# Five small loads into an unread tile, in a decode layer with attention and an MLP

## The chip, the cores and the metric

The kernel runs on one core of a Trainium2 chip, with one launch. The metric is device time in microseconds (us); the figure for the kernel before is the median of three runs. Beside them stands one execution that the hardware profiler recorded. Engines are TensorE (PE; its weight loads are PEld), VectorE (DVE), ScalarE (ACT), GpSimd (POOL) and SyncE (SP). SP and ACT issue the DMAs of this kernel; a "q" behind an engine's name (SPq) means its instruction queue.

## What is computed

One token `x` of width 1024 is normalised, and then goes two ways whose results are added to it: attention over the last 4096 positions of a cache, with 32 query heads on 4 key/value heads, and an MLP of width 3584.

```python
xn  = layernorm(x)                                   # 1 x 1024
q   = xn @ wq                                        # 1024 x 4096
p   = softmax(q . k_cache[last 4096] * 128**-0.5)    # 32 heads, 4 kv heads
o   = (p . v_cache[last 4096]).reshape(1, 4096)
a   = o @ wo                                         # 4096 x 1024
b   = gelu(layernorm(xn) @ w1 + b1) @ w2 + b2        # 1024 x 3584, 3584 x 1024
out = x + a + b
```

With one token every weight is used once. In bf16 the caches, `wq`, `wo`, `w1` and `w2` come to nearly 40 MB, all of which must be loaded.

## The kernel before

All large operands go through four SBUF buffers of 32 KB per partition (`ring`, lines 56 to 64). SP issues their loads in this order: `k_sb` in four loads (line 72), `wq` in two (81), `w1` in two (207), `v_sb` in three (213), `w2` in two (221), `wo` in six (229). The first half of `wo` is one load of 16 rows for each partition; the second half is cut into 8, 4, 2, 1 and 1 rows, so that the last rows can be used one by one. ACT issues three small loads at the start (lines 102 to 104): `x`, `b2` and `b1`, each into a single partition. A load from `w1` on can be issued only when a buffer has been released by the work that read it.

The work follows the loads. DVE transposes the keys in blocks (186); DVE and ACT copy them in order (200, 202); PE makes `q` (238), the MLP's first layer (258), the scores (276) and the attention output (320). Then 56 matmuls of `w2` and 56 of `wo` accumulate in PSUM (341). The last four rows of `wo` (lines 350 to 359) go into two other accumulators, `acct`, while ACT and DVE copy out the sum so far (345, 346); that sum is added back partly by PE (353) and partly by DVE (361). Two stores of 1 KB each, one issued by SP (364) and one by ACT (365), end the kernel.

Two things set the order around the change. The first is a planner, which orders each engine's instructions. It simulates the program with its own costs, and on each engine takes, among the instructions that are ready in the simulation, the one that stands first in the source. An instruction that needs nothing can so come to run before others that stand above it, unless it is tied to one (`issue_after`, line 101). Line 349 shows it: its two clears of `acct` stand in the source behind the copies of lines 345 and 346, and run 22 us before them.

The second is the completion counters. The planner gives every DMA one of eight counters, which I number 0 to 7, in turn, in the planned order over both queues. A DMA may be issued only when the DMA that had its counter before it has landed; where nothing else makes that certain, a wait is put in front of it. In the program before, the 22 loads take the counters 0 to 7, 0 to 7 and 0 to 5. The store by ACT then takes counter 6 and the store by SP counter 7. At the end of the program (line 391) SP waits for everything by a list of five wait instructions with two conditions each, and a drain behind them. The list stands in the order of the counters from the middle outward: counters 3 and 2; 4 and 1; 5 and 0; 6 and DVE; 7 and ACT. When it is through, all engines meet at a barrier and the kernel ends.

Of the kernel before, what the change touches and what calls it, by code (L numbers as in the profile page):

```python
# [9 lines left out]
BF16 = mybir.dt.bfloat16  # L10
# [6 lines left out]
def kernel(  # L17
# [14 lines left out]
    nc = tc.nc  # L32
# [21 lines left out]
    consts = ctx.enter_context(tc.tile_pool(name="consts", bufs=1))  # L54
# [135 lines left out]
    for g in range(Hkv):  # L190
        T4 = scr[:, g, :].rearrange("p (c a j) -> p c a j", a=4, j=32)
        k = 0
# [30 lines left out]
    wo_v = A_wo.rearrange("(p c) n -> p c n", p=P)  # L223
    for i, cuts in enumerate([[0, 16], [0, 8, 12, 14, 15, 16]]):
# [4 lines left out]
            nc.sync.dma_start(out=tv[:, a:b, :], in_=wo_v[:, nr * i + a:nr * i + b, :])  # L229
        chunk_src += [("o", nr * i + r, tv[:, r, :]) for r in range(nr)]  # L230


    for i, w3 in enumerate(wq_tiles):
        for r in range(4):
# [161 lines left out]
```

## Time and profile before

| | |
|---|---|
| timed runs | 101.76, 101.72, 101.69 us; median 101.72 us |
| profiled execution, first to last instruction (span) | 100.0 us |
| its own time | the page gives the span alone; with the 1.7 us that the median has beyond it, 101.72 us |
| busy: PE, PEld, DVE, ACT, POOL | 51.2, 20.0, 49.7, 34.1, 3.8 us |
| moved by DMA | 39.92 MB in 2878 packets, 399 GB/s over the span |

A row of DMA digits on the page gives, in 40 slices of 2.5 us, the mean busy share of the 16 DMA engines in tenths; 9 means 90% or more. The chain of waits follows the work that ended last back from the end. In the queue's waits, "SPq L81 <- DMA k_sb" is the time for which SP's queue stood at line 81 until a load of `k_sb` had landed.

### The profile page before, as it was taken

The numbers are of one execution on the slowest core, as the hardware profiler recorded it, in microseconds if no ns is written. First come the engines' busy times: TensorE is split into PE (matmuls) and PEld (weight loads), VectorE is DVE, ScalarE is ACT, GpSimd is POOL, SyncE is SP. The second block draws the span as 40 slices with busy tenths as digits, with TensorE's granted clock in tenths as the row PEclk, the third lists the DMA queues.
The fourth block names the chain that finished last, engine by engine and source line by source line (L and its number), as shares of the span: only waits on it lengthen the run. The fifth ranks groups of instructions, "written<-read, shape, count | busy, mean of one in ns | idle before, by whom it ended". The sixth has DMA issues, their size and how long they took to land.

```text
span 100.0 us, 970 instructions
## 1 busy us (share of the span) xinstructions
PE 51.2 (51%) x365; PEld 20.0 (20%) x365; DVE 49.7 (50%) x92; ACT 34.1 (34%) x37; POOL 3.8 (4%) x16
## 2 busy tenths in 40 slices
PE   0065200008500940193892935999469950199980
PEld 0042200002100310031530322334123410033320
DVE  5445499999999999997125115410450000000021
ACT  5000002999999999962001044400000000000010
POOL 6005200000000000000000000000000000000000
PEclk9999999999995579555555555559985998557999
DMA  2999999999999999998999999999999999999920
GB/s 26 394 420 426 491 488 472 419 419 419 432 419 393 401 500 382 413 482 378 390 429 426 429 531 390 413 477 390 459 447 426 419 432 419 406 419 411 401 73 1
DMA packets 2878, 39.92 MB, mean 399 GB/s; under 512 B 309, under 2 KB 311, under 8 KB 698
## 3 DMA queue, kind: packets, MB, share of 16 engines
q1 hardware_dynamic: 2866, 39.85, 93.6%
q8 instruction: 3, 0.05, 0.2%
q10 hardware_dynamic: 8, 0.01, 0.0%
q14 instruction: 1, 0.01, 0.0%
HBM read 39.86 MB, written 0.00 MB: 398 GB/s over the span
## 4 chain that ended last, share of the span: by engine, by line
DVE 38%; DMA 24%; PE 21%; issue 9%; POOL 3%; ACT 2%; SPq 1%; POOLq 1%; ACTq 0%
DMA wo<-in_A_wo_dram 24%; DVE kt_scr L186 17%; DVE kT L202 16%; PE o_all L320 10%; PE sp L276 4%; PE acch L258 3%; ACT e L298 1%; DVE eTb L300 1%; PE qT_ps L262 1%; DVE m_loc L284 1%; PE acct L357 1%; SPq L229 1%; DVE q_sb L241 1%; POOLq L391 1%; POOL spread L110 1%
## 5 line engine op out<-in xcount | busy, mean ns | idle before, releaser
L200 ACT COPY kT<-kt_scr 32x1024 bf16<-32x1024 bf16 x26 | 27.1, 1042 | 14.8 <-DVE kt_scr L186 14.5
L186 DVE STREAM_TRANSPOSE kt_scr<-k_sb 128x4096 bf16<-128x4096 bf16 x4 | 17.4, 4411 | 0.0
L238 PE MATMUL accq<-wq,xnT 128*1 128x512 bf16 x64 | 7.1, 622 | 18.3 <-DMA wq<-in_A_wq_dram 18.3
L202 DVE COPY kT<-kt_scr 32x1024 bf16<-32x1024 bf16 x38 | 15.9, 419 | 0.5
L346 DVE COPY bulk<-accf 33x320 f32<-33x320 f32 x1 | 0.5, 483 | 21.9 <-ACT bulk L345 21.9
L341 PE MATMUL accf<-wo,o 128*1 128x512 bf16 x56 | 8.3, 459 | 6.0 <-DMA wo<-in_A_wo_dram 5.9
L345 ACT COPY bulk<-accf 33x192 f32<-33x192 f32 x1 | 0.3, 312 | 31.9 <-PE accf L341 31.9
L320 PE MATMUL o_all<-v_sb,eTb 128*32 128x512 bf16 x32 | 10.0, 491 | 1.0 <-DVE zcol L311 1.0
L258 PE MATMUL acch<-w,yT 128*1 128x448 bf16 x64 | 6.3, 572 | 6.0 <-DMA w<-in_B_w_dram 6.0
L341 PE MATMUL accf<-w,hT 128*1 128x512 bf16 x56 | 7.9, 451 | 0.0
L238 PEld LDWEIGHTS <-xnT 128*1 128x1 bf16 x64 | 2.1, 116 | 22.5 <-issue 22.4
L320 PEld LDWEIGHTS <-eTb 128*32 128x32 bf16 x32 | 3.8, 120 | 6.9 <-issue 3.9
L341 PEld LDWEIGHTS <-o 128*1 128x1 bf16 x56 | 2.8, 97 | 11.4 <-issue 9.2
L258 PEld LDWEIGHTS <-yT 128*1 128x1 bf16 x64 | 2.0, 115 | 9.8 <-issue 9.8
L276 PE MATMUL sp<-kT,qm 128*32 128x512 bf16 x32 | 3.8, 630 | 0.3 <-DVE qm L267 0.3
L341 PEld LDWEIGHTS <-hT 128*1 128x1 bf16 x56 | 2.7, 96 | 4.7 <-issue 2.5
L323 DVE TENSOR_TENSOR o_m<-o_all,grs 32x512 f32<-32x512 f32 x1 | 0.7, 680 | 5.8 <-PE o_all L320 5.8
L123 PE MATMUL x_ps<-ones_bf,xb 1*128 1x1 bf16 x8 | 0.7, 200 | 5.0 <-DMA xb<-in_A_x_dram 5.0
L298 ACT ACTIVATE e<-sc,nmx 128x1024 bf16<-128x1024 f32 x1 | 1.1, 1148 | 5.7 <-DVE nmx L295 5.7
L315 DVE STREAM_TRANSPOSE hT<-h_sb 128x896 bf16<-128x896 bf16 x1 | 1.7, 1706 | 2.4 <-ACT h_sb L313 2.4
L276 PEld LDWEIGHTS <-qm 128*32 128x32 bf16 x32 | 2.1, 133 | 1.4 <-issue 0.9
L281 ACT COPY sc<-sp 128x512 f32<-128x512 f32 x1 | 0.6, 585 | 4.8 <-PE sp L276 4.8
(88 smaller groups left out, 35.9 us busy)
## 6 DMA issues: line engine op xcount, KB each, us to landing
w<-in_B_w_dram SPq DMA_DIRECT2D x4, 3584.0 KB
wq<-in_A_wq_dram SPq DMA_DIRECT2D x2, 4096.0 KB, 27.0
k_sb<-in_A_k_cache_dram SPq DMA_DIRECT2D x4, 1024.0 KB, 7.1
wo<-in_A_wo_dram SPq DMA_DIRECT2D x1, 4096.0 KB, 29.4
v_sb<-in_A_v_cache_dram SPq DMA_DIRECT2D x1, 2048.0 KB, 19.2
v_sb<-in_A_v_cache_dram SPq DMA_DIRECT2D x2, 1024.0 KB, 23.1
wo<-in_A_wo_dram SPq DMA_DIRECT2D x1, 2048.0 KB
wo<-in_A_wo_dram SPq DMA_DIRECT2D x1, 1024.0 KB
```

Of the source, the lines that this page charges most:

```text
L110: nc.gpsimd.affine_select(out=spread[:], in_=spread[:], compare_op=ALU.not_equal, fill=1.0, base=0, pattern=[[-1, 4], [1, P]], channel_mul ...
L186: nc.vector.transpose(out=scr[:, g, :], in_=k2[:, g, :])
L200: nc.scalar.copy(out=dst, in_=src)
L202: nc.vector.tensor_copy(out=dst, in_=src)
L229: nc.sync.dma_start(out=tv[:, a:b, :], in_=wo_v[:, nr * i + a:nr * i + b, :])
L238: nc.tensor.matmul(accq[32 * t:32 * t + 1, b, :], lhsT=xnT[:, c:c + 1], rhs=w3[:, r, j * 512:(j + 1) * 512], start=(c == 0), stop=(c == C ...
L258: nc.tensor.matmul(acch[32 * t:32 * t + 1, b, :NH], lhsT=yT[:, c:c + 1], rhs=w3[:, r, j * NH:(j + 1) * NH], start=False, stop=(c == C - 1) ...
L276: nc.tensor.matmul(sp[32 * R:32 * R + 32, :], lhsT=qm[:, g, :], rhs=kT[:, g, c0:c0 + 512], start=(g == 0), stop=(g == Hkv - 1), tile_posit ...
L298: nc.scalar.activation(out=e128[:], in_=sc[:], func=ACT.Exp, bias=nmx[:], scale=scale, accum_out=l_loc[:])
L315: nc.vector.transpose(out=hT[:], in_=h_sb[:].rearrange("p (d c) -> p c d", c=CW2))
L320: nc.tensor.matmul(o_all[:].rearrange("h g d -> h (g d)"), lhsT=eTb[:, 32 * c:32 * c + 32], rhs=v4[:, :, c, :], start=(c == 0), stop=(c == ...
L341: nc.tensor.matmul(accf[32 * half:32 * half + 1, :], lhsT=vec[kind](c), rhs=wap[:, half * 512:(half + 1) * 512], start=False, stop=(idx == ...
```

## The change

Behind the loops that issue `wo`, a tile `marks` of 16 partitions and 1536 bf16 columns (3 KB in each partition) is added, and five loads into it, which SP issues. They take 7, 9, 11, 13 and 15 partitions and 78, 82, 86, 90 and 94 columns: 156 to 188 bytes for each partition, 55 pieces in all, some 9.6 KB. Each goes into columns of its own, and nothing reads the tile. The source is the head of `wo`: in each partition, the first columns of the first row that it holds. Nothing else is changed.

```diff
@@ -229,6 +229,11 @@
             nc.sync.dma_start(out=tv[:, a:b, :], in_=wo_v[:, nr * i + a:nr * i + b, :])
         chunk_src += [("o", nr * i + r, tv[:, r, :]) for r in range(nr)]
 
+    marks = consts.tile([16, 1536], BF16)
+    for k in (7, 9, 11, 13, 15):
+        w = 64 + 2 * k
+        nc.sync.dma_start(out=marks[0:k, 96 * k:96 * k + w], in_=wo_v[0:k, 0, 0:w])
+
 
     for i, w3 in enumerate(wq_tiles):
         for r in range(4):
```

## The prediction, made before the result was known

> **What bounds the kernel now.** I read the page first: which engine is never idle?
>
> ```profile
> span 100.0 us, 970 instructions
> ...
> DMA  2999999999999999998999999999999999999920
> ...
> DMA packets 2878, 39.92 MB, mean 399 GB/s; under 512 B 309, under 2 KB 311, under 8 KB 698
> ...
> q1 hardware_dynamic: 2866, 39.85, 93.6%
> q8 instruction: 3, 0.05, 0.2%
> ```
>
> It is the DMA: nine tenths or more in nearly every slice from 2.5 us to 95 us, while no compute engine is over 51% busy. The third line also tells how a load is made up. Nineteen loads go to 128 partitions, five transfers (three loads, two stores) touch one. 19 x 16 + 5 = 309, the number of packets under 512 B: a full load ends with one tiny packet on each of 16 DMA engines, a transfer of one partition with one. These tiny packets raise the completion counter.
>
> Next, how the stream ends, in the busy time by stage (the last two columns are the DMA's share of 16 engines and GB/s):
>
> ```profile
> 26.50:95.00 68.50, 41.72 (x287) 15.89 (x288) 28.85 (x63) 22.34 (x24) 0.00 (x0) 0.68 1.00 427
> ...
> 95.50:96.00 0.50, 0.30 (x6) 0.17 (x6) 0.03 (x1) 0.31 (x1) 0.00 (x0) 1.00 0.34 111
> 96.00:96.50 0.50, 0.50 (x12) 0.18 (x8) 0.46 (x1) 0.00 (x0) 0.00 (x0) 1.00 0.13 49
> 96.50:97.00 0.50, 0.50 (x8) 0.17 (x5) 0.00 (x0) 0.00 (x0) 0.00 (x0) 1.00 0.02 8
> ```
>
> The 16 engines don't end together. A share of 0.34 is some five engines, 0.13 is two, and 0.02 is one engine for 0.16 us (0.02 x 16 x 0.5). A load has landed only when its last engine is through, so one straggler sets the end.
>
> Then the chain of waits in order of time, from 95 us:
>
> ```profile
> 72.11 23.63 DMA wo<-in_A_wo_dram
> 95.74 0.04 issue
> 95.79 0.60 PE acct L357 x8
> 96.39 0.42 PE acct L353 x4
> 96.81 0.55 PE acct L357 x6
> 97.36 0.02 issue
> 97.38 0.48 DVE res L361
> ```
>
> Behind the landing of `wo` rows 12 and 13 stands a fixed tail: 1.6 us of PE, 0.5 us of DVE. Whatever delays the straggler delays the end one for one.
>
> Last, SP's queue: its longest waits, then the finishing list of line 391 (from two short windows: operation, count, ns min/median/max, first and last start):
>
> ```profile
> SPq L364 <- DVE res L361: 24.4, 1, 24.4
> SPq L207 <- DMA wq<-in_A_wq_dram: 16.9, 1, 16.9
> ...
> SPq L81 <- DMA k_sb<-in_A_k_cache_dram: 2.3, 1, 2.3
> ```
> ```profile
> L391 SPq EVENT_SEMAPHORE  x3: 28/28/28, 98.3 to 98.4; - x3
> ```
> ```profile
> L391 SPq EVENT_SEMAPHORE  x1: 28/28/28, 99.2 to 99.2; - x1
> L391 SPq DRAIN  x1: 7/7/7, 99.3 to 99.3; - x1
> ```
>
> The third wait shows the counters going round: the second `wq` load needs a fresh buffer and no data, yet it waits for the first `k_sb` load, which had its counter eight DMAs before. The list shows what a satisfied wait costs: the first three pass at 98.29, 98.35 and 98.42, 63 ns apart, as their loads are long done. The fourth stands until ACT's store has landed (99.04), the fifth until SP's has (99.22), and the drain follows 65 ns later.
>
> **The change part by part.**
>
> *Where the loads run.* They need no buffer of the ring and no data, so in the planner's simulation they are ready at once. SP has nothing else to issue while it waits for 16.9 us in front of line 207, so I expect them there, behind `wq` and far ahead of `wo`. Five issues at 0.33 to 0.70 us, the range of SP's plain issues early on, are 1.7 to 3.5 us. On the counters they follow `x`, `b2`, `k_sb`'s second, `b1` and `k_sb`'s third load, all landed by 11 us. The gap that hides them lasts to 22.9 us: nothing. If they stay where the source has them, SP's wait of 24.4 us covers them, though three must wait for earlier parts of `wo` on their counters: the last for the cut of four rows, landed by 94.5 us. Issue and landing then end near 97 us, and SP is needed at 97.93: nothing again. No real load gets a late wait: each moves on by five counters, to predecessors that landed at least 3 us before its issue time.
>
> *The finishing list.* In either place five DMAs more stand ahead of the stores, so ACT's store moves from counter 6 to 11 - 8 = 3 and SP's from 7 to 4. The list begins with counters 3 and 2, then 4 and 1. SP's store, the last to land, is now awaited second of five instead of fifth. Behind its landing still stand the waits for 5 and 0, for 6 and DVE, for 7 and ACT: 3 x 63 ns = **0.19 us** that used to pass while the stores were in flight. All engines meet behind SP, so nothing covers it. From below this is zero, if the order of the list follows something other than the counter's number; from above 4 x 63 ns = 0.25 us, if SP's store is awaited first.
>
> *The packets in the stream.* 9.6 KB at 399 GB/s is 0.02 us spread evenly, but what counts is the straggler's share. It gets between none and five of the loads. A load's piece of 156 to 188 bytes was never recorded before. The trace's packet records have 9 ns for the 4 bytes of a completion and 44 ns for a store of 1 KB; a row of 2 KB takes 84 ns. On the line between the first two 172 bytes are 15 ns, and with its completion 24 ns. I take this, as the nearest rows by size. Five would be 0.12 us; with 55 pieces on 16 engines the mean is 3.4, so **0.08 us**. The ends are 0 (straggler without pieces) and 5 x (84 + 9) ns = 0.47 us (each as dear as a whole 2 KB row). A gain is possible too, if the straggler changes (below).
>
> The Trainium skill, "DMA: Bandwidth & Descriptors", section "Why a DMA increments its semaphore by 16 and not by 1", says that a load uses the largest number of engines up to 16 that divides its partitions, and always the lowest-numbered. By that, seven engines get all five pieces and one gets none, and the straggler costs 0.12 us or nothing instead of 0.08. The view doesn't name the straggler, so I keep the mean.
>
> *The rest.* The tile takes 3 KB of each partition and shifts buffers behind it; no row prices that, and with the DMA as the bound I take nothing (inside the bounds). Planned orders of PE, DVE and ACT may change a little, which hides behind the stream: `w1`, the tightest, is issued at 26.5 us with `wq` in flight till 32.6.
>
> Sum: 101.72 + 0.19 + 0.08 = **101.99 us**. The terms are from one execution of 100.0 us span, taken as the median with its 1.72 us outside.
>
> **Rivals.** 0.2% or 0.20 us is about what a measurement of this kernel can tell from no change.
>
> *Not slower: the finishing list doesn't lengthen.* Its order could follow the planned landing, or counters might be given otherwise, so that the last wait is again for a store. Against it stands only that all waits of the program before go by number. Price of the list 0; with 0.02 to 0.08 for packets 101.74 to 101.80. It decides if the list adds under 0.12 us (0.20 less 0.08 for packets), that is, if at least two of its three waits vanish.
>
> *The list alone.* The straggler gets no piece, or the loads stay behind `wo`'s last row. For the second speaks the source; against it line 349, whose clears run far ahead of what stands above them. 101.91, just within 0.2%.
>
> *Dear packets.* If odd, short pieces cost as much as a 2 KB row or more, the stream grows by up to 0.47 us: 102.1 to 102.4. Against it: the completions of 4 bytes, 16 for each load, leave the stream at 427 GB/s. But these carry no data. The Trainium skill, same page, section "Specifications", has under 512 B a read-modify-write, which speaks for this rival; it gives no time for it, and no run here shows one.
>
> *Another straggler.* Three packets of instructions (16 KB each, q8) go through the same engines; 16 KB is 0.66 us of one engine at 399/16 GB/s. Shifted pieces may move such a packet to an engine with slack. The next engine ends about 0.16 us sooner (the 0.02 above), so the stream gains that at most: 101.75 with the list, 101.56 without.
>
> **How the numbers follow.** My forecast 0.46 (its own range 101.93 to 102.09), the list alone 0.16, no longer list 0.14, dear packets 0.12, another straggler 0.12. Slower by over 0.2% (above 101.92): forecast and dear packets, 0.58. Within 0.2%: the list alone, the unchanged list and most of the straggler, 0.33. Faster: 0.09, the straggler with the list unchanged or a gain no row shows. The range runs from 101.72, where only the faster cases and a little of the unchanged list fall out, to 102.34, just short of the dear end (101.72 + 0.19 + 0.47 = 102.38).
>
> **What would show it.** The five issues at SP between 6 and 12 us; three waits of line 391 and their 63 ns steps behind SP's last store, and the drain 0.25 us instead of 0.065 behind that store's wait; `wo`'s last landings less than 0.15 us later. I am wrong if the last wait of the list is still a store's, if the end of the stream moves by over 0.2 us either way, or if SP reaches line 207 or 364 late.

## The result

| | before | after |
|---|---|---|
| median, 5 runs each | 101.76 us (101.69 to 101.86) | 102.08 us (102.03 to 102.29) |
| ratio after to before | | 1.0036, 95% interval [1.0022, 1.0051] |
| profiled span | 100.0 us | 100.4 us |

The change makes the kernel 0.32 us slower by the medians. The forecast was 101.99 us from a base of 101.72, that is +0.27 us. Two later sets of 12 runs of the same kernel gave ratios of 1.0026 [1.0012, 1.0041] and 1.0025 [1.0014, 1.0037], +0.26 and +0.24 us by the medians. So +0.24 to +0.32 us has to be explained.

The lines of the page of after that answer to those shown of before:

```profile
span 100.4 us, 975 instructions
...
DMA  2999999999999998999899998999989999999910
...
DMA packets 2988, 39.93 MB, mean 398 GB/s; under 512 B 419, under 2 KB 421, under 8 KB 808
...
q1 hardware_dynamic: 2976, 39.86, 93.3%
q8 instruction: 3, 0.05, 0.2%
```

The DMA is still the bound. There are 110 packets more, all under 512 B: 55 pieces and 55 completions. A load of 7 partitions so ends with 7 completions, not 16. This agrees with the Trainium skill, "DMA: Bandwidth & Descriptors", section "Why a DMA increments its semaphore by 16 and not by 1": the number of engines is the largest up to 16 that divides the partitions.

SP's queue shows where the loads run. First its instructions of lines 235 and 369 in order of time (start, us, line), then its waits there (total, times, longest):

```profile
72.28 22.63 SPq L235 DMA_DIRECT2D marks<-in_A_wo_dram  x5
98.05 0.24 SPq L369 DMA_DIRECT2D out_dram<-res  x1
```
```profile
SPq L235 <- DMA wo<-in_A_wo_dram: 16.0, 3, 9.4
...
SPq L235 <- DMA w<-in_B_w_dram: 5.0, 1, 5.0
...
SPq L369 <- DVE res L366: 3.1, 1, 3.1
```

They run behind the last row of `wo`, where the source has them, and not behind `wq`. Three wait for parts of `wo`, one for the second half of `w2`, each for the load that had its counter before. The last is issued at 94.59 us. SP then still stands 3.1 us until `res` is ready: these waits cost nothing.

The chain of after, in order of time from 95 us, and the last stages of the stream (the DMA's share is the last column but one; from 95.46 us on the added loads land there too):

```profile
94.82 1.29 PE accf L346 x12
96.11 0.44 PE acct L362 x8
96.55 0.46 PE acct L358 x4
97.01 0.47 PE acct L362 x6
97.48 0.02 issue
97.50 0.48 DVE res L366
```
```profile
95.50:96.00 0.50, 0.50 (x8) 0.22 (x6) 0.00 (x0) 0.00 (x0) 0.00 (x0) 1.00 0.23 79
96.00:96.50 0.50, 0.50 (x10) 0.21 (x6) 0.00 (x0) 0.31 (x1) 0.00 (x0) 1.00 0.26 83
96.50:97.00 0.50, 0.50 (x8) 0.15 (x8) 0.48 (x1) 0.00 (x0) 0.00 (x0) 1.00 0.05 18
```

`res` is ready 0.12 us later than in the execution of before. By the trace's landing times 0.08 us of that is the last row of `wo`, which landed at 97.08 us against 97.00. The rest is PE, which stands last in the chain here: from 91 to 93 us its granted clock was 0.60, against 0.97 in the execution of before, and its matmuls of `wo` (line 346) took 490 ns on the average, against 459. Neither belongs to the change: the kernel before, profiled again, has its last row at 97.18 us, a clock of 0.50 in that window, and `res` 0.60 us later than in its first profile. Another execution of the same kernel, profiled later, has the chain of before again and `res` 0.05 us earlier than there:

```profile
71.25 24.43 DMA wo<-in_A_wo_dram
95.68 0.04 issue
95.72 0.60 PE acct L362 x8
96.32 0.42 PE acct L358 x4
96.74 0.57 PE acct L362 x6
97.31 0.02 issue
97.33 0.48 DVE res L366
```

Its span is 100.25 us all the same, 0.22 us over that of before's first profile. What is left lies behind the stores: the finishing list. Here are its five waits and the drain, in the first execution of after (operation, count, ns min/median/max, first and last start):

```profile
L396 SPq EVENT_SEMAPHORE  x5: 28/28/28, 99.3 to 99.6; - x5
L396 SPq DRAIN  x1: 7/7/7, 99.7 to 99.7; - x1
```

and the same waits of before, in one window:

```profile
L391 SPq EVENT_SEMAPHORE  x5: 28/28/28, 98.3 to 99.2; - x5
L391 SPq DRAIN  x1: 7/7/7, 99.3 to 99.3; - x1
```

Before, the list was worked through from 98.3 us on, and its first three waits passed while the stores were in flight. After, its first wait stands until 99.34 us, and all the others follow behind it. The trace's landing times make this exact. Before, the last store landed at 99.200 us and the drain came at 99.282, 82 ns later. After, the last landing was at 99.327 and the drain at 99.661, 334 ns later. That is 0.25 us more.

### The profile page after: what moved, and what is told of

Same layout as the page of the kernel before. It is cut to its first block, busy times and chain, and to the rows that moved or that the text cites. A ratio compares the mean times of both kernels' runs of the same rounds, so it can differ in the third digit from the quotient of the medians.

```text
span 100.4 us, 975 instructions
## 1 busy us (share of the span) xinstructions
PE 50.0 (50%) x365; PEld 19.8 (20%) x365; DVE 49.7 (50%) x92; ACT 34.1 (34%) x37; POOL 3.8 (4%) x16
## 4 chain that ended last, share of the span: by engine, by line
DVE 36%; DMA 30%; PE 18%; issue 9%; POOL 3%; POOLq 1%; ACT 1%
DMA wo<-in_A_wo_dram 30%; DVE kt_scr L186 17%; DVE kT L202 16%; PE accf L346 9%; PE sp L281 4%; PE acch L263 2%; DVE m_loc L289 1%; PE qT_ps L267 1%; PE acct L362 1%; DVE q_sb L246 1%; POOLq L396 1%; POOL spread L110 1%; ACT sc L286 1%; POOL rstd L145 1%; DVE res L366 0%
## 5 line engine op out<-in xcount | busy, mean ns | idle before, releaser
L346 PE MATMUL accf<-wo,o 128*1 128x512 bf16 x56 | 8.8, 490 | 6.5 <-DMA wo<-in_A_wo_dram 6.5
L325 PE MATMUL o_all<-v_sb,eTb 128*32 128x512 bf16 x32 | 9.4, 464 | 1.6 <-DMA v_sb<-in_A_v_cache_dram 1.6
L263 PE MATMUL acch<-w,yT 128*1 128x448 bf16 x64 | 5.5, 514 | 6.2 <-DMA w<-in_B_w_dram 6.2
```

The costliest lines, as they stand in the source:

```text
L263: nc.tensor.matmul(acch[32 * t:32 * t + 1, b, :NH], lhsT=yT[:, c:c + 1], rhs=w3[:, r, j * NH:(j + 1) * NH], start=False, stop=(c == C - 1) ...
L325: nc.tensor.matmul(o_all[:].rearrange("h g d -> h (g d)"), lhsT=eTb[:, 32 * c:32 * c + 32], rhs=v4[:, :, c, :], start=(c == 0), stop=(c == ...
L346: nc.tensor.matmul(accf[32 * half:32 * half + 1, :], lhsT=vec[kind](c), rhs=wap[:, half * 512:(half + 1) * 512], start=False, stop=(idx == ...
```

## The experiments

Two theories. The **list theory**: five DMAs more move the stores from counters 6 and 7 to 3 and 4, early in the list, and the waits behind theirs are no longer hidden. The **pieces theory**: the loads cost the time themselves, by their short, odd pieces or by their place near the end.

### The changed kernel again

> The changed kernel once more, beside the others on one chip. Both theories: 0.3 to 0.4 us over the kernel before. The list theory (the stores moved to counters 3 and 4, so that waits for other counters stand behind theirs in SP's finishing list): 0.25 to 0.35 us between the last landing of a store and the drain behind the list, against 0.08 us before.

102.07 against 101.81 us, ratio 1.0026 [1.0012, 1.0041]; 269 ns from the last landing to the drain. The time, +0.26 us, is a little under the 0.3 us that both expected; the 269 ns are the list theory's. This time SP's store landed last, in the first profile it was ACT's. That explains 269 against 334: ACT's wait (counter 3) is the first of the list and SP's (counter 4) the second.

### Three loads more, to bring the counters round

```diff
     kt_scr = ring_tile("kt_scr")
+    early = consts.tile([1, 384], BF16)
+    for k in range(3):
+        nc.sync.dma_start(out=early[:, 128 * k:128 * k + 78], in_=A_wo[k:k + 1, 0:78])
```

added to the changed kernel.

> The five loads, and three more of one partition behind wq: eight DMAs more, so that the counters come round and the stores are on 6 and 7 again, as in the kernel before. List theory: the 0.25 us go, the drain follows the last store's landing within 0.15 us, and the time is that of the kernel before, plus 0.0 to 0.1 us. Pieces theory (the 55 short, odd pieces or the five loads themselves cost the time): all that the change costs stays, 0.3 us or more over the kernel before.

The list came out as the list theory has it, 143 ns. The time did not: 102.10 against 101.81 us, ratio 1.0023 [1.0007, 1.0039], as slow as the changed kernel. In its profile `wo`'s last row landed 0.22 us later than in that of before. Taken alone this set speaks for the pieces theory, or for a second cause; it was repeated, below.

### Only the three early loads

The same three lines, added to the kernel before.

> Only the three loads of one partition behind wq, none behind wo: the stores move to counters 1 and 2, which stand in the second and the first place of the list. List theory: 0.19 to 0.25 us over the kernel before, nearly as much as the change, though three pieces are loaded in place of 55 and none near the end. Pieces theory: 0.0 to 0.05 us.

101.98 against 101.81 us, ratio 1.0015 [1.0002, 1.0029]: +0.17 us by the medians, and 311 ns from landing to drain, 229 ns more than before. With three pieces, all in the middle of the stream, most of the change's cost is there. The pieces theory had 0.05 us at most. The time alone doesn't exclude that, as its interval begins at 0.02 us; the 229 ns in the trace, which that theory doesn't have, do.

### Five loads of one partition each

```diff
-        nc.sync.dma_start(out=marks[0:k, 96 * k:96 * k + w], in_=wo_v[0:k, 0, 0:w])
+        nc.sync.dma_start(out=marks[0:1, 96 * k:96 * k + w], in_=wo_v[0:1, 0, 0:w])
```

> The five loads where they are, of one partition each: 5 pieces in place of 55, the counters as in the changed kernel. List theory: as the changed kernel, within 0.1 us. Pieces theory: a fifth of the change's cost or less, under 0.1 us over the kernel before.

102.09 against 101.81 us, ratio 1.0026 [1.0008, 1.0044], and 334 ns: with 5 pieces in place of 55 the cost is the same. No part of it that shows hangs on the number or the shape of the pieces.

### The kernel before against itself

> The kernel before, unchanged, timed as if it were a change: how far two sets of runs of one program stand apart. Every theory: 0.0 us, within 0.1 us; the drain of the list 0.08 or 0.14 us behind the last store's landing, by which store lands last. If it comes out 0.15 us or more off, the 0.2 us that the kernel with eight loads was slower than the list theory said need no cause.

101.85 against 101.78 us, ratio 1.0003 [0.9985, 1.0021], and 81 ns. One program compared with itself so has an interval of 0.18% to either side, and its profiled execution had `wo`'s last landing 0.19 us later than the first profile of before. A shift of 0.2 us of the stream in one profile tells nothing.

### Eight loads, second set

The kernel with three early loads and the five behind `wo` again.

> The five loads and three early ones again, with the stores back on counters 6 and 7. List theory alone: 0.0 to 0.1 us over the kernel before. If the five loads behind wo have a cost of their own beside the list: 0.15 to 0.3 us once more, and the trace should show stores issued or landing later against the last landing of wo.

101.86 against 101.78 us, ratio 1.0008 [0.9995, 1.0021]; 144 ns. No cost of its own showed, as the list theory says.

### The tile without the loads

```diff
+    marks = consts.tile([16, 1536], BF16)
+    nc.gpsimd.memset(marks[0:1, 0:2], 0.0)
```

in place of the change.

> The tile without the loads: GpSimd clears two elements of it, so that it keeps its 3 KB in each partition and the buffers behind it move as in the changed kernel; no DMA is added. List theory: 0.0 us, within 0.1 us. If the moved buffers cost something: 0.1 to 0.2 us, with the stream ending later.

101.84 against 101.78 us, ratio 1.0005 [0.9994, 1.0017]; 82 ns. The moved buffers cost nothing that shows.

### The loads behind `wq`

The five loads (with a copy of the line that makes `wo_v`) moved in the source to just behind `kt_scr = ring_tile("kt_scr")`.

> The same five loads behind wq in the source, where the prediction had thought them to run; the stores are on counters 3 and 4 all the same. List theory: 0.19 to 0.25 us from the list, as in the changed kernel, and the 55 pieces in the middle of the stream add 0.0 to 0.1 us: 0.2 to 0.35 us in all. Pieces theory, by which only pieces near the end or only short odd pieces count: near 0.0 us if it is their place, 0.3 us if it is their shape, with the drain of the list then no later than in the kernel before.

102.16 against 101.78 us, ratio 1.0034 [1.0017, 1.0051]; 269 ns, with SP's store landing last. SP's instructions in order of time, between 2 and 27 us, and the list:

```profile
...
2.85 3.19 SPq L81 DMA_DIRECT2D wq<-in_A_wq_dram  x2
6.08 5.12 SPq L88 DMA_DIRECT2D marks<-in_A_wo_dram  x5
26.68 0.36 SPq L212 DMA_DIRECT2D w<-in_B_w_dram  x1
```
```profile
L396 SPq EVENT_SEMAPHORE  x5: 27/28/28, 98.9 to 99.2; - x5
L396 SPq DRAIN  x1: 7/7/7, 99.3 to 99.3; - x1
```

Here the loads do run where the prediction had thought, from 6 to 11 us in front of `w1`'s first, and the cost is that of the change or somewhat more: +0.38 us by the medians, just above the 0.35 us that the list theory had as its upper end. That their place doesn't matter is shown for the list. `wo`'s last row landed at 96.80 us, no later than in before (97.00), but this profile is of the fastest of the 12 runs (101.75 us). So it shows no mark of the 55 pieces on the stream's end, and the set of runs doesn't exclude 0.1 us for them.

### One early load alone

The three lines of above with `range(1)`, added to the kernel before.

> One load of one partition behind wq and none behind wo: the stores move to counters 7 (ACT) and 0 (SP), the fifth and the third place of the list. List theory, with SP's store landing last as in the kernel before: two more waits stand behind its own, so the drain comes 0.08 + 2 x 0.063 = 0.21 us behind the landing; 0.08 us if ACT's lands last. Pieces theory: 0.08 us as before.

186 ns from SP's landing to the drain, where 208 were expected (82 + 2 x 63) and 82 by the pieces theory. The wait for the store passed 22 ns sooner behind the landing than in the changed kernel, as with three early loads (311 ns); why isn't known. The one time, 101.95 us, is too little to read.

### The changed kernel and the one with eight loads, side by side

The third set of runs of each, on one chip.

> The changed kernel, third set of runs, beside the one with eight loads on one chip. List theory: 0.25 to 0.4 us over the kernel before, and 0.12 to 0.25 us over the kernel with eight loads.

> The five loads with three early ones, stores back on counters 6 and 7, third set of runs; the first two lay 0.29 and 0.08 us over the kernel before. List theory: 0.0 to 0.15 us over the kernel before, and under the changed kernel. Pieces theory: as the changed kernel, or above it.

The changed kernel: 102.09 us, ratio 1.0025 [1.0014, 1.0037], 333 ns. The same five loads with three more ahead: 101.87 us, ratio 1.0000 [0.9990, 1.0009], 143 ns. The kernel before: 101.85 us. The list of the kernel with eight loads, in the trace:

```profile
L399 SPq EVENT_SEMAPHORE  x5: 28/28/28, 98.2 to 99.3; - x5
L399 SPq DRAIN  x1: 7/7/7, 99.4 to 99.4; - x1
```

It begins at 98.2 us again, with the stores in flight. Three small loads more take away the cost of five: 0.22 us between the medians, 0.19 us by the lists (333 less 143 ns). Over all sets, by the means, the kernel with eight loads is 0.11 us slower than before (three sets: 0.24, 0.08 and 0.01) and the changed kernel 0.28 us (the two sets of 12: 0.30 and 0.26). The difference of 0.17 us is again about that of the lists. With the traces this speaks for the list; the first set of the kernel with eight loads stays the exception.

All profiled executions together:

| kernel | counters of the stores, ACT / SP | last to land | waits of the list behind its wait | landing to drain |
|---|---|---|---|---|
| before; before again; tile only | 6 / 7 | SP | 0 | 82; 81; 82 ns |
| eight loads, three sets | 6 / 7 | ACT | 1 | 143; 144; 143 ns |
| one early | 7 / 0 | SP | 2 | 186 ns |
| after, 2nd set; loads behind `wq` | 3 / 4 | SP | 3 | 269; 269 ns |
| three early | 1 / 2 | SP | 4 | 311 ns |
| after, 1st and 3rd set; five of one partition | 3 / 4 | ACT | 4 | 334; 333; 334 ns |

The time from the later of the two store issues to the later landing is 1.26 to 1.27 us in all of them but one (1.32 in the second set of after), and from the drain to the end of the span it is 0.75 us in all. The list is what differs.

The way to the stores doesn't. In ten of the 13 executions `res` is ready 866 to 869 ns behind the landing of `wo`'s last row. In the other three PE was late, by 0.04 and 0.23 us (after, 1st and 2nd set) and by 0.41 us (before again). The last row landed at 97.02 us on the average of the five executions without the five loads (96.92 to 97.18), and at 97.04 us on that of the seven with the loads behind `wo` (96.95 to 97.21). So these loads didn't move the stream's end by anything that shows.

In times, the kernels of the last three rows with more than one run were 0.17 to 0.38 us slower than before by their medians, those of the first two rows 0.02 to 0.08 us, with one exception: the first set of the kernel with eight loads (+0.29 us). Its cause isn't known. The list was short in it, and two further sets didn't repeat it.

## Why the prediction was right, point by point

**The bound and the fixed tail.** Right: the end of the stream is as before, and the way from `wo`'s last row to `res` is fixed unless PE is late. The tail was read a little off: the view puts 1.6 us of PE behind rows 12 and 13, landed at 95.74 us, but the straggler's end at 97.00 us is the last row, and only 0.87 us stand behind that.

**Where the loads run.** Wrong. Line 349 had been read as a sign that the planner would move the loads up to SP's gap behind `wq`. It did not: in both places that were tried, behind `wo` and behind `wq`, SP issues its loads in the order of the source. A load that waits for a buffer seems to hold what stands behind it on that queue (these two orders are all that shows it); clears on another engine told nothing of this. The text had priced the other place too ("nothing again"), and the waits for `wo`'s cuts ended at 94.6 us, as it had said of the cut of four rows (94.5).

**The finishing list.** Right in mechanism: the stores went to counters 3 and 4, and waits for other counters stood behind theirs. The term was 0.19 us for three waits of 63 ns; it measured 0.19 us where SP's store landed last (269 less 82 ns) and 0.25 us where ACT's did (334 less 82). The prediction had only SP's landing last in mind; 0.25 us was its upper end, for another reason. With the stores on these counters and five loads directly ahead of SP's, three of the four profiled executions had ACT's last. SP's own issue took 243 ns in all four, against 307 in before.

**The packets in the stream.** The term that failed, 0.08 us. By the step on the place the pieces should have been in the stream. They were issued behind the last load of `wo` instead and landed from 95.46 us on, when the first engines had ended their share of it (95.28), and the stream's end stayed where it was. With the loads behind `wq` the pieces were in the stream, but that set of runs can't tell 0.08 us from nothing. The size for one piece was close: 15 ns was read off the line between neighbours, and the trace's packet records have 13 to 15 ns for 156 to 188 bytes (one of 55 took 38). That speaks against dear packets, the rival for which the Trainium skill's "DMA: Bandwidth & Descriptors", section "Specifications", was named: if there was a read-modify-write under 512 B, these records don't show its price.

**The sum.** +0.27 us was forecast, +0.24 to +0.32 measured. That it came out so near is partly luck: 0.08 us too much for packets stood where up to 0.06 us were missing from the list. The list explains 0.19 to 0.25 us. What may be left beyond it, up to 0.1 us, has no cause here; the kernel before against itself was 0.07 us apart.

**The rivals.** "The list doesn't lengthen" is excluded by the trace. "The list alone" was closest in mechanism; its 0.19 us were up to 0.06 us short. "Dear packets" falls by the packet records, 13 to 15 ns against 84 for a row of 2 KB, also with the loads behind `wq`, where all 55 took 14 or 15 ns; the single-partition loads, which cost the same, agree. "Another straggler" is not seen: the stream's end moves by 0.2 us between executions of one program, so a gain of 0.16 us couldn't be told from that in one profile, and the averages above differ by 0.02 us.

## What to carry to other kernels

The end of a program is a serial list too. When DMAs are handed counters in turn and the finish waits for the counters in a fixed order, the number of DMAs ahead of the final stores decides how much of that list is hidden behind them; count it modulo the number of counters. A small slowdown of a change that "does nothing" should be looked for there before it is put down to the transfers. And where a few tenths of a per cent count, time the kernel against itself once: the spread of that comparison says which differences need a cause.

## What had not been expected of the hardware

Which of the two stores lands last, though they are issued 12 to 14 ns apart by two queues, isn't fixed: SP's in all six profiles with no load just ahead of SP's store, ACT's in six of the seven with such loads. The pair takes 1.26 to 1.27 us in either order, and 1.32 us once. And one of the pieces was slow: in the first profile of after the load of 15 partitions was issued at 94.59 us and landed at 98.19, while that of 13 partitions, issued at 92.13 us, landed at 97.11; a packet of instructions was moved at 96.2 us and took until 97.14. In two profiles of the kernel with eight loads (the first and third set) the same load was late too, and in all three it landed 1.05 us behind the end of such a packet. That may be the reason, but this was not tried. It still landed about a microsecond ahead of the stores.
